# Score units as steps of their own, raw products of the first pair ahead of its maxima, and a new table of numbers behind a planned schedule

## The chip, the cores and the metric

The kernel runs on one core of one Trainium2 chip. The metric is device time in microseconds (us) of one execution; lower is better. A profiled execution also gives a trace of every engine: PE is TensorE (PEld its weight loads), DVE is VectorE, ACT is ScalarE, POOL is GpSimd, SP is the engine from whose queue nearly all DMAs are issued.

## The reference, cut to what matters

Three stages follow each other, all in float32, with B=4, H=8 heads, S=576, D=64, d_model 512, d_ff 1024:

```
scores = q @ k.T / 8, masked by blocks of 64 (block_i >= block_j)
attn   = exp(scores - max) / (sum + 1e-9);   x = attn @ v          # per head
h      = relu(x @ w_in);  conv over time with 3 taps per channel
x      = (h * sigmoid(conv)) @ w_out                               # first feed-forward stage
h      = relu(x @ w_in2); u, v = halves;  v_n = layer norm of v
x      = (u * (w_spatial @ v_n + b_spatial)) @ w_out2              # second feed-forward stage
```

## The kernel before

Heads are worked in 16 pairs, four to a batch. For a pair p these steps run on PE, and each leaves a task for the other engines:

- `max_step` (line 519, four per pair): rounded products of keys and queries in whole-array matmuls, only to find each row's maximum; DVE reduces them from PSUM into `mx` (lines 535 and 542). `max_tr` (line 555) turns `mx` over; the result is copied to `mt` (line 567 on ACT or 569 on DVE) and sent by two small DMAs into row 0 of each half of `mq` (line 574).
- `score` (line 635): the exact products again, with PE divided into two halves of 64 rows, one per head. `unit` (line 600) makes one PSUM tile: for the first six pairs (`PF32`) float32 products of `raw` (line 613), later three products of split values `kp`, `qbd`, `kl` (line 621), and on top a product of `mk` and `mq` (line 625) that subtracts the maxima and masks. ACT takes the exponential into `e` (line 629). Two calls of `score` per pair make two units each.
- `av` (line 647): products with `v` and with ones, in the divided array (line 323). `norm_b` (line 742) spreads the reciprocal of the sums; DVE multiplies (line 753), POOL rounds the result to `x` (line 326) and the rest goes to the second half of `x` (line 329 on DVE, 333 on POOL).
- `in1` and `out1` (lines 769 and 814): the first feed-forward stage, whole-array matmuls of line 315, in tiles of 12 to 24. ACT, DVE and POOL turn each `in1` tile into a gate `g` (lines 788 to 805); `out1` leaves `y`, which goes out to memory and comes back for the second stage.

Every float32 operand of a whole-array matmul is split into a rounded high part and a low part, the low part being a subtraction: `minus` (line 331) makes it on DVE or on POOL. Weights arrive as 64-bit words and are rebuilt first: `words_to_f32` (line 384) takes the sign on DVE (line 392) or on POOL (line 390), then two shifts on DVE (394, 396); `split64` (line 399) loads and splits one weight unit of 128x512.

The order of all of this is planned when the program is built. `Order` (line 88) plays the engines through time with assumed durations (`t_act`, `t_dve`, `t_round`, `t_ptt`) and instructions stand on each engine in the order in which this play starts them. Whenever its PE is free, `pick_at` (line 896) chooses the next step: maxima, `norm_b`, attention steps or the feed-forward stream, by how far the two streams have come (`AHEAD`). PSUM has three double banks `st` and two single banks `mo` in this phase. A table of numbers at lines 30 to 77 sets thresholds, priorities (`P_...`), start times of the weight loads (`PREP_...`) and bit masks; in a mask, bit p or bit c says which engine takes the work of pair p, weight unit c or tile c.

When attention is done its buffers close, the second stage's weights `w2i` load and are split, and the second stage runs (lines 1028 to 1250).

Of the kernel before, what the change touches and what calls it, by code (L numbers as in the profile page):

```python
# [38 lines left out]
X1KEEP = (1, 2)
PONES = 7  # L40
KL_POOL = 0x4018
QL_POOL = 0x8038
SGN_POOL = 0xf500
M_ACT = 0x9000
Q_DVE = 0x1180
PTWO = 16
P_KL = 1
# [10 lines left out]
EARLY_M = 5
TILE_ON = 0.2
JOIN = 0  # L60
S_FIRST = 6
# [209 lines left out]


def t_round(n):
    return 0.11 + n * 0.00092


def t_ptt(n):
    return 0.15 + n * 0.0021


@with_exitstack
def attn_moe_moe2_kernel(
# [98 lines left out]
    qbd = [att.tile([128, NBLK, 128], F32R, name=f"qbd{i}") for i in range(NKP)]  # L381


    def words_to_f32(r, f, prio, pool=False):
        n = f.shape[-1]
        yield ("ACT", t_act(n, False), lambda: nc.scalar.activation(
            f, r[:, :, 1].bitcast(F32), ACTF.Copy, scale=2.0 ** -112), 0, prio)
        if pool:
            s = r[:, :, 1].bitcast(F32)
            yield ("POOL", t_round(n), lambda: nc.gpsimd.tensor_scalar(s, s, 0.0, None, ALU.mult), 0, prio)  # L390
        else:
            yield ("DVE", t_dve(n, True), lambda: nc.vector.tensor_scalar(
                r[:, :, 1], r[:, :, 1], 0x80000000, None, ALU.bitwise_and), 0, prio, True)
# [4 lines left out]

    def split64(src, hi, lo, key, pool=None, prio=None):
        prio = P_W if prio is None else prio  # L400
        unit = {"w1i": 0, "w1o": 8, "w2i": 16, "w2o": 24}[key[0]] + key[-1] + (4 * key[1] if len(key) > 2 else 0)
# [13 lines left out]
        yield from words_to_f32(r, f, prio, (SGN_POOL >> unit) & 1)  # L415
# [219 lines left out]
    def score(p, g):
        def fn():
            ES[p, g] = att.tile([128, 2, ESZ[g]], F32, name=f"e{g}", tag=f"e{g}", bufs=NE[g])
            if g == 0 and p >= PONES:
                od.spawn(add_up(p), "att")
            tasks = [unit(p, g, i) for i in range(2)]  # L640
            if g == 1 and p >= PF32:
# [778 lines left out]
```

## Time and profile before

| | us |
|---|---|
| median of 3 runs (lowest, highest) | 625.69 (624.18, 626.79) |
| the profiled execution, its device time | 625.44 |
| the profiled execution, span from first to last instruction | 623.7 |
| PE busy in the span | 584.6 |
| DVE, ACT, POOL busy | 469.5, 255.4, 149.2 |

The span and the busy times belong to the profiled execution; 1.7 us of its device time lie outside the span. A busy engine is one with an instruction in flight. PE's matmuls overlap, so short gaps between them do not show as idle.

### The profile page before, as it was taken

The numbers are of one execution on the slowest core, as the hardware profiler recorded it, in microseconds if no ns is written. First come the engines' busy times: TensorE is split into PE (matmuls) and PEld (weight loads), VectorE is DVE, ScalarE is ACT, GpSimd is POOL, SyncE is SP. The second block draws the span as 40 slices with busy tenths as digits, with TensorE's granted clock in tenths as the row PEclk, the third lists the DMA queues.
The fourth block names the chain that finished last, engine by engine and source line by source line (L and its number), as shares of the span: only waits on it lengthen the run. The fifth ranks groups of instructions, "written<-read, shape, count | busy, mean of one in ns | idle before, by whom it ended". The sixth has DMA issues, their size and how long they took to land.

```text
span 623.7 us, 12021 instructions
## 1 busy us (share of the span) xinstructions
PE 584.6 (94%) x4638; PEld 524.4 (84%) x4638; DVE 469.5 (75%) x1010; ACT 255.4 (41%) x516; POOL 149.2 (24%) x202
## 2 busy tenths in 40 slices
PE   5888799899999999999999999799999999999997
PEld 4655578798879978979788999798889999998997
DVE  6799979796987967969948498888794577258257
ACT  4556554633524715527336273636333013103101
POOL 6012133430351201306242130222121122012011
PEclk9999999999999999999999999999999999999999
DMA  5656521313121023040010285435700600510012
GB/s 172 196 173 189 175 79 30 127 39 102 41 96 61 2 98 99 2 136 3 23 58 21 75 257 145 134 102 153 228 1 16 215 20 0 173 56 2 1 58 76
DMA packets 41927, 56.65 MB, mean 91 GB/s; under 512 B 9381, under 2 KB 34725, under 8 KB 41870
## 3 DMA queue, kind: packets, MB, share of 16 engines
q1 hardware_dynamic: 41182, 55.69, 28.4%
q8 instruction: 36, 0.59, 0.4%
q0 software_dynamic: 400, 0.16, 0.1%
q14 instruction: 21, 0.17, 0.1%
q10 hardware_dynamic: 288, 0.04, 0.0%
HBM read 41.42 MB, written 14.16 MB: 89 GB/s over the span
## 4 chain that ended last, share of the span: by engine, by line
PE 49%; DVE 28%; DMA 8%; issue 7%; POOL 4%; ACT 3%; SPq 1%; ACTq 0%; POOLq 0%; DVEq 0%
PE mo L315 27%; PE st L315 12%; PE st L323 5%; DVE cc L795 5%; DVE mx L542 4%; DVE cc L800 3%; DVE es L689 2%; DVE kl L329 2%; DVE g L329 2%; DMA w_raw<-in_w2i_dram 2%; PE st L621 2%; PE st L613 2%; DMA w_raw<-in_w1o_dram 2%; DMA w_raw<-in_w1i_dram 2%; POOL g L326 1%
## 5 line engine op out<-in xcount | busy, mean ns | idle before, releaser
L315 PE MATMUL mo<-x,w1i_h 128*128 128x290 f32 x488 | 105.5, 300 | 4.9 <-ACT h L788 4.1
L315 PE MATMUL mo<-g,w1o_h 128*128 128x288 f32 x416 | 89.9, 299 | 2.6 <-DVE y L833 2.6
L315 PEld LDWEIGHTS mo<-x,w1i_h 128*128 128x128 f32 x488 | 80.9, 189 | 7.3 <-ACT h L788 5.1
L326 POOL TENSOR_SCALAR g<-cc 128x288 fp32r<-128x288 f32 x64 | 38.7, 608 | 186.2 <-DVE cc L800 178.5
L795 DVE SCALAR_TENSOR_TENSOR cc<-h,cwt,cc 128x288 f32<-128x288 f32 x128 | 67.2, 539 | 8.6 <-ACT cc L792 8.0
L315 PEld LDWEIGHTS mo<-g,w1o_h 128*128 128x128 f32 x416 | 68.8, 189 | 5.5 <-DVE y L833 3.9
L315 PE MATMUL mo<-x,w1i_l 128*128 128x290 f32 x244 | 72.4, 297 | 0.0
L315 PE MATMUL mo<-g,w1o_l 128*128 128x288 f32 x208 | 61.4, 295 | 0.0
L629 ACT ACTIVATE e<-st 128x640 f32<-128x640 f32 (+1 forms) x64 | 50.8, 833 | 17.6 <-PE st L625 9.9
L323 PE MATMUL st<-e,v 128*64 128x448 f32 (+4 forms) x384 | 48.4, 402 | 7.0 <-DVE mx L542 5.1
L315 PE MATMUL mo<-x,w2i_h 128*128 128x288 f32 x256 | 52.6, 296 | 1.6 <-ACT u L1092 1.5
L323 PEld LDWEIGHTS st<-e,v 128*64 128x64 f32 x384 | 25.5, 139 | 31.7 <-issue 16.6
L326 POOL TENSOR_SCALAR gt<-ga 128x288 fp32r<-128x288 f32 x40 | 21.0, 524 | 116.2 <-DVE ga L1117 74.2
L542 DVE TENSOR_REDUCE mx<-st 128x1 f32<-128x320 f32 (+6 forms) x100 | 44.8, 483 | 3.0 <-PE st L315 2.8
L315 PEld LDWEIGHTS mo<-x,w1i_l 128*128 128x128 f32 x244 | 46.1, 189 | 0.1
L315 PEld LDWEIGHTS mo<-x,w2i_h 128*128 128x128 f32 x256 | 41.4, 188 | 2.7 <-ACT u L1092 2.6
L792 ACT ACTIVATE cc<-h,cwt 128x288 f32<-128x288 f32 x64 | 33.6, 535 | 18.4 <-DVE g L329 14.3
L315 PE MATMUL mo<-ws_h,vnh 128*128 128x288 f32 x135 | 39.6, 297 | 1.4 <-issue 1.1
L797 ACT ACTIVATE cc<-cc 128x288 f32<-128x288 f32 x64 | 27.8, 441 | 31.8 <-DVE cc L795 30.8
L329 DVE TENSOR_TENSOR gt<-ga,gt 128x288 fp32r<-128x288 f32 x56 | 25.0, 468 | 19.8 <-POOL gt L326 19.8
L315 PE MATMUL st<-w2i_h,x 128*128 128x512 f32 x128 | 39.5, 390 | 0.0
L315 PEld LDWEIGHTS mo<-g,w1o_l 128*128 128x128 f32 x208 | 39.1, 188 | 0.1
(168 smaller groups left out, 1460.3 us busy)
## 6 DMA issues: line engine op xcount, KB each, us to landing
x2d<-y SPq DMA_DIRECT2D x32, 288.0 KB
x<-x2d SPq DMA_DIRECT2D x16, 576.0 KB
raw<-in_kq_dram SPq DMA_DIRECT2D x15, 576.0 KB
v<-in_vt_dram SPq DMA_DIRECT2D x16, 320.0 KB
out_dram<-o SPq DMA_DIRECT2D x32, 144.0 KB
w_raw<-in_w1i_dram SPq DMA_DIRECT2D x8, 512.0 KB
w_raw<-in_w1o_dram SPq DMA_DIRECT2D x8, 512.0 KB
w_raw<-in_w2i_dram SPq DMA_DIRECT2D x8, 512.0 KB
```

The lines of the kernel that those rows point to most:

```text
L315: nc.tensor.matmul(o, w, x, start=start, stop=stop)
L323: nc.tensor.matmul(o[row:row + m], w, x, start=start, stop=stop)
L326: nc.gpsimd.tensor_scalar(o, i, 1.0, 0.0, ALU.mult, ALU.add)
L329: nc.vector.tensor_tensor(o, a, b, ALU.subtract)
L542: yield ("DVE", t_dve(n), lambda: nc.vector.tensor_reduce(mx[:, c:c + 1], st[bk][:, o:o + n], AX.X, ALU.max), 0, 0)
L613: nc.tensor.matmul(out, keys(RAW[p][:, 0, :], r), RAW[p][r, 1, q0:q0 + nq], start=True, stop=False)
L621: nc.tensor.matmul(st[:, e, o:o + nq], keys(kx, slice(64 * e, 64 * e + 64)), qx[e], start=j == 0, stop=False)
L629: yield ("ACT", t_act(2 * n), lambda: nc.scalar.activation(ex[:, :, e0:e0 + n], st[:, :, 0:n], ACTF.Exp, scale=0.125), 0, 0)
L792: yield ("ACT", t_act(HT, False, 1), lambda: nc.scalar.activation(cc, h[:, o:o + HT], ACTF.Copy, scale=cwt[:, c, 1:2]), 0, P_G)
L795: yield ("DVE", t_dve(HT, ptr=1), lambda: nc.vector.scalar_tensor_tensor(cc, h[:, o + e:o + e + HT], cwt[:, c, j:j + 1], cc, ALU.mult, ALU ...
L797: yield ("ACT", t_act(HT, False), lambda: nc.scalar.activation(cc, cc, ACTF.Tanh, scale=0.5), 0, P_G)
L800: yield ("DVE", t_dve(HT), lambda: nc.vector.scalar_tensor_tensor(cc, cc, 1.0, h[:, o:o + HT], ALU.add, ALU.mult), 0, P_G, True)
```

## The change

1. `score` makes one unit per step instead of two, so that `pick_at` can put another step between the two units of a call.
2. For pair 0 the first two units are cut in two: their raw products (line 613 before) are a step that needs only the loaded data, the product with the maxima is a second step.
3. `stay`: when PE is in the divided array and an attention step lacks nothing but a PSUM bank or its margin, the planner waits up to `STICK` = 0.1 us for it.
4. The planner's durations of ACT and POOL work are changed.
5. Almost the whole table of numbers is new: which engine takes which work, priorities, when weights load, how the streams are interleaved.

```diff
-AHEAD = (0.58, 0.27, 0.16, 0.37)
-PREP_AT = 18
+AHEAD = (0.47, 0.62, 0.22, 0.75)
+PREP_AT = 8
...
-W_DVE = 0xffffff7
+W_DVE = 0x6fd08
...
 def t_round(n):
-    return 0.11 + n * 0.00092
+    return 0.317 + n * 0.00056
 def t_ptt(n):
-    return 0.15 + n * 0.0021
+    return 0.31 + n * 0.0019
...
-    def unit(p, g, i):
+    HALF = {}
+    def unit(p, g, i, part=None):
         n, parts, et, e0 = SSTEPS[g][i]
         q, ex = mq[p % NQ], ES[p, et]
-        st = two_banks()
+        st = HALF.pop((p, g, i)) if part == 1 else two_banks()
+        if part == 0:
+            HALF[p, g, i] = st
...
-                if p < PF32:
+                if p < PF32 and part != 1:
                     nc.tensor.matmul(out, keys(RAW[p][:, 0, :], r), RAW[p][r, 1, q0:q0 + nq], start=True, stop=False)
...
-            for e in range(2):
+            for e in range(2 if part != 0 else 0):
                 r = slice(64 * e, 64 * e + 64)
                 nc.tensor.matmul(st[:, e, o:o + nq], keys(mk, r), q[r, q0:q0 + nq], start=False, stop=True)
...
-    def score(p, g):
+    def score(p, g, i, part=None):
...
+        if part == 0:
+            return dict(needs=[("raw", 0, 0), ("raw", 0, 1)], rings=[("st", 1)] + ([(f"e{g}", 1)] if i == 0 else []), fn=fn, tile=True)
+        if part == 1:
+            return dict(needs=[("m", p)], rings=[], fn=fn, tile=True)
...
+        if p == 0:
+            sstream.extend(score(p, 0, i, part) for part in range(2) for i in range(2))
+        sstream.extend(score(p, g, i) for g in range(p == 0, 2) for i in range(2))
...
+    def stay():
+        if not od.tile or od.t - od.pe_free >= STICK:
+            return False
+        if ready("v", vstream, 0.0) or ready("s", sstream, 0.0) or not (due("s", sstream) or due("v", vstream)):
+            return False
+        od.push(od.t + 0.05, lambda: None)
+        return True
...
     def pick():
+        if stay():
+            return None
```

Three places show what this does to the order.

The first is PE from the end of pair 0's maxima. `mo` and `st` are PSUM tiles, `qbd_97` and `qbd_98` the queries of pairs 0 and 1, `raw` the loaded data, `ident` marks the turning of the maxima. Before:

```order
L315 MATMUL st<-kp,qbd_97 128x288 x2
L561 MATMUL st<-ident,mx 9x128
L315 MATMUL mo<-kp,qbd_98 128x64
L315 MATMUL mo<-kp,qbd_98 128x128
L315 MATMUL mo<-kp,qbd_98 128x192
L315 MATMUL mo<-kp,qbd_98 128x256
L315 MATMUL st<-kp,qbd_98 128x320
L315 MATMUL st<-kp,qbd_98 128x384
L315 MATMUL st<-kp,qbd_98 128x448
L315 MATMUL st<-kp,qbd_98 128x512
L613 MATMUL st<-raw 128x320 x2
L625 MATMUL st<-mq_94,mk 128x320 x2
```

Now:

```order
L619 MATMUL st<-raw 128x320 x2
L316 MATMUL st<-kp,qbd_97 128x320
L316 MATMUL st<-kp,qbd_97 128x384
L619 MATMUL st<-raw 128x256 x2
L316 MATMUL mo<-kp,qbd_97 128x448
L316 MATMUL mo<-kp,qbd_97 128x512
L316 MATMUL st<-kp,qbd_97 128x288 x2
L562 MATMUL st<-ident,mx 9x128
```

Two pairs of raw products have moved from behind eight products of pair 1 to a place ahead of the turning of pair 0's maxima.

The second is POOL after its first copies. `qbd` are rounded queries, `x` the rounded attention output of a pair, `w_raw` the sign of a weight unit, `w1i_l` and `w1o_l` low parts of weights. Before:

```order
L333 TENSOR_TENSOR w1i_l<-w_f,w1i_h 128x4x128
L326 TENSOR_SCALAR x_538<-xpair 128x576
L326 TENSOR_SCALAR qbd_98<-raw 64x9x64
L326 TENSOR_SCALAR x_700<-xpair 128x576
L390 TENSOR_SCALAR w_raw<-w_raw 128x512
L326 TENSOR_SCALAR qbd_97<-raw 64x9x64
L326 TENSOR_SCALAR x_859<-xpair 128x576
L390 TENSOR_SCALAR w_raw<-w_raw 128x512 x2
L326 TENSOR_SCALAR x_1018<-xpair 128x576
L390 TENSOR_SCALAR w_raw<-w_raw 128x512 x2
```

Now:

```order
L391 TENSOR_SCALAR w_raw<-w_raw 128x512
L334 TENSOR_TENSOR w1i_l<-w_f,w1i_h 128x4x128 x2
L327 TENSOR_SCALAR qbd_98<-raw 64x9x64
L334 TENSOR_TENSOR w1i_l<-w_f,w1i_h 128x4x128 x2
L327 TENSOR_SCALAR qbd_97<-raw 64x9x64
L334 TENSOR_TENSOR w1i_l<-w_f,w1i_h 128x4x128 x2
L327 TENSOR_SCALAR x_557<-xpair 128x576
L327 TENSOR_SCALAR qbd_98<-raw 64x9x64
L334 TENSOR_TENSOR w1i_l<-w_f,w1i_h 128x4x128
L327 TENSOR_SCALAR x_707<-xpair 128x576
L334 TENSOR_TENSOR w1o_l<-w_f,w1o_h 128x512
```

The subtractions of seven `w1i` units and one `w1o` unit stand on POOL where one stood, and the signs have gone back to DVE but for one.

The third is SP's queue behind the first loads. `mq_94` and `mq_95` are the rows of maxima of pairs 0 and 1. Before:

```order
L949 DMA cwr<-in_cw_dram 128x48
L511 DMA v<-in_vt_dram 128x640 x2
L574 DMA mq_94<-mt 1x9x64
L459 DMA raw<-in_kq_dram 128x1152
L411 DMA w_raw<-in_w1i_dram 128x4x256
L574 DMA mq_95<-mt 1x9x64
```

Now:

```order
L982 DMA cwr<-in_cw_dram 128x48
L512 DMA v<-in_vt_dram 128x640
L412 DMA w_raw<-in_w1i_dram 128x4x256
L512 DMA v<-in_vt_dram 128x640
L575 DMA mq_94<-mt 1x9x64
L412 DMA w_raw<-in_w1i_dram 128x4x256 x2
L460 DMA raw<-in_kq_dram 128x1152
L412 DMA w_raw<-in_w1i_dram 128x4x256
L575 DMA mq_95<-mt 1x9x64
```

Four loads of weights are issued ahead of the second pair's row of maxima, where one was.

## Rows read from the trace of the kernel before

**Rows 1.** The page's span, and its first part: busy us, share, instructions.

```profile
span 623.7 us, 12021 instructions
...
PE 584.6 (94%) x4638; PEld 524.4 (84%) x4638; DVE 469.5 (75%) x1010; ACT 255.4 (41%) x516; POOL 149.2 (24%) x202
```

**Rows 2.** Windows: stretch, length, busy us (instructions) per engine, clock, DMA share, GB/s.

```profile
0.00:15.00 15.00, 8.08 (x32) 6.21 (x33) 10.38 (x29) 6.54 (x12) 9.46 (x20) 1.00 0.53 179
15.00:75.00 60.00, 48.77 (x513) 34.48 (x514) 53.06 (x124) 35.72 (x55) 9.58 (x10) 1.00 0.59 177
75.00:120.00 45.00, 42.02 (x428) 33.47 (x424) 36.52 (x76) 25.00 (x48) 13.86 (x12) 0.96 0.31 100
120.00:345.00 225.00, 217.77 (x1828) 193.45 (x1829) 181.45 (x363) 101.09 (x204) 65.31 (x79) 1.00 0.17 54
345.00:480.00 135.00, 128.00 (x868) 121.37 (x867) 104.83 (x225) 62.83 (x141) 28.17 (x40) 1.00 0.42 127
480.00:624.00 144.00, 139.93 (x978) 135.43 (x977) 83.27 (x195) 24.20 (x58) 22.85 (x42) 1.00 0.21 67
```

**Rows 3.** PE's waits from 15 to 75: total us, times, longest.

```profile
PE st L323 <- DVE mx L542: 4.4, 3, 1.6
PE st L315 <- ACT e L629: 3.1, 3, 1.2
PE st L315 <- DVE mt L569: 1.6, 1, 1.6
PE st L323 <- ACT e L629: 1.4, 2, 1.0
```

**Rows 4.** PE's waits from 75 to 345.

```profile
PE mo L315 <- DVE y L833: 2.6, 5, 0.8
PE st L315 <- DVE srow L714: 2.2, 1, 2.2
...
PE st L561 <- DVE mx L542: 0.9, 1, 0.9
```

**Rows 5.** PE's waits from 345 to 480.

```profile
PE mo L315 <- ACT h L788: 3.2, 2, 1.8
...
PE mo L315 <- DVE y L833: 0.8, 1, 0.8
```

**Rows 6.** DVE, timeline at the start: start, us, instruction, idle before it.

```profile
18.14 0.28 DVE L569 CAST mt<-st 9x128 fp32r<-9x128 f32 x1 [1.91 <-PE st L561]
...
23.94 0.44 DVE L392 TENSOR_SCALAR w_raw<-w_raw 128x512 uint32<-128x512 uint32 x1 [1.96 <-ACT w_f L386]
```

**Rows 7.** Groups by form: busy us, mean ns of one, idle before.

```profile
L329 DVE TENSOR_TENSOR g<-cc,g 128x288 fp32r<-128x288 f32 x52 | 29.7, 576 | 6.5 <-POOL g L326 6.4
...
L333 POOL TENSOR_TENSOR g<-cc,g 128x288 fp32r<-128x288 f32 x12 | 11.5, 955 | 0.9
...
L390 POOL TENSOR_SCALAR w_raw<-w_raw 128x512 f32<-128x512 f32 x6 | 10.4, 1740 | 15.6 <-ACT w_f L386 15.6
...
L392 DVE TENSOR_SCALAR w_raw<-w_raw 128x512 uint32<-128x512 uint32 x22 | 10.2, 463 | 7.8 <-ACT w_f L386 7.6
...
L329 DVE TENSOR_TENSOR kl<-raw,kp 128x576 fp32r<-128x576 f32 x9 | 8.7, 965 | 0.1
...
L329 DVE TENSOR_TENSOR w1i_l<-w_f,w1i_h 128x512 fp32r<-128x512 f32 x7 | 4.8, 683 | 0.2 <-ACT w1i_h L420 0.2
...
L333 POOL TENSOR_TENSOR kl<-raw,qbd 64x576 fp32r<-64x576 f32 x2 | 3.4, 1702 | 0.2
```

**Rows 8.** POOL alone, groups by form.

```profile
L333 POOL TENSOR_TENSOR w1i_l<-w_f,w1i_h 128x512 fp32r<-128x512 f32 x1 | 1.3, 1277 | 3.7 <-ACT w1i_h L420 3.7
```

**Rows 9.** The tile `g`: shortest, median and longest ns of DVE's subtraction.

```profile
L329 DVE TENSOR_TENSOR g<-cc,g x52: 432/452/2375, 100.8 to 406.0; 128x288 fp32r<-128x288 f32 x52
```

**Rows 10.** DVE's waits over the span, for the sign of weights on POOL.

```profile
DVE w_raw L394 <- POOL w_raw L390: 7.1, 3, 2.7
```

**Rows 11.** SP's queue at 307 us: the issue of one row of maxima.

```profile
307.11 0.76 SPq L574 DMA_DIRECT2D mq<-mt  x1
```

More of the change, by code (lines that the diff above doesn't have):

```diff
@@ L29 @@
 NEG = -(2.0 ** 30)
-AHEAD = (0.58, 0.27, 0.16, 0.37)
-PREP_AT = 18
+AHEAD = (0.47, 0.62, 0.22, 0.75)
+PREP_AT = 8
 PREP_DT = 2.5
-PREP_DT2 = 5
-PREP_AT2 = 46
+PREP_DT2 = 2.5
+PREP_AT2 = 36
 NKP = 2
@@ L38 @@
 PF32 = 6
-X1KEEP = (1, 2)
+X1KEEP = (0, 1)
 PONES = 7
[L41 to L47, printed above, removed]
+KL_POOL = 0xbe22
+QL_POOL = 0xaa37
+SGN_POOL = 0x1
+M_ACT = 0xd8c6
+Q_DVE = 0x0
+PTWO = 5
+P_KL = 2
 NPR = 0
 SPLIT = 2
-GLO_POOL = (192, 197, 0, 36, 8, 129, 64, 0)
-W_DVE = 0xffffff7
-P_KPQ, P_RAW, P_V, P_G, P_W = 1, 0, 1, 1, 3
-X1_POOL = 0x10a0
-CWP = 0
+GLO_POOL = (225, 117, 200, 165, 56, 76, 104, 144)
+W_DVE = 0x6fd08
+P_KPQ, P_RAW, P_V, P_G, P_W = 0, 0, 1, -1, 2
+X1_POOL = 0x8328
+CWP = 1
 NX1 = 6
@@ L57 @@
 NRAW = 3
[L58 to L61, printed above, removed]
+EARLY_M = 2
+TILE_ON = 0.3
+JOIN = 0.01
+S_FIRST = 2
 HOLD = 1
-STKEEP = 0
+STKEEP = 2
 MARGIN = 0.4
-EARLY = 2
-WPRIO = 3
+STICK = 0.1
+EARLY = 3
+WPRIO = 1
 W2PRIO = 2
-W2DT = 2.0
+W2DT = 0.8
 DMA_LAG = 0.8
-ADD_DVE = 0xbfff
-V_ACT = 0xdcfd
-S_ACT = 0x6214
+ADD_DVE = 0xffca
+V_ACT = 0xa77d
+S_ACT = 0x258a
 P_ADD = 0
-XE = (1.0, 2.25)
+XE = (0.5, 1.75)
 XMO = 7
-XK = 0.4
+XK = 0.25
 WR = 2
@@ L158, in enqueue @@
         eng, dur, fn = it[:3]
-        lat = it[3] if len(it) > 3 else 0.0
+        lat = (it[3] if len(it) > 3 else 0.0) + (0.03 if eng == "ACT" else 0.0)
         prio = it[4] if len(it) > 4 else 1
@@ L381, in attn_moe_moe2_kernel, with words_to_f32 @@
     qbd = [att.tile([128, NBLK, 128], F32R, name=f"qbd{i}") for i in range(NKP)]
-    def words_to_f32(r, f, prio, pool=False):
+    def words_to_f32(r, f, prio, sign="DVE"):
         n = f.shape[-1]
-        yield ("ACT", t_act(n, False), lambda: nc.scalar.activation(
+        yield ("ACT", t_act(n, False) + 0.04, lambda: nc.scalar.activation(
             f, r[:, :, 1].bitcast(F32), ACTF.Copy, scale=2.0 ** -112), 0, prio)
-        if pool:
-            s = r[:, :, 1].bitcast(F32)
-            yield ("POOL", t_round(n), lambda: nc.gpsimd.tensor_scalar(s, s, 0.0, None, ALU.mult), 0, prio)
+        s = r[:, :, 1].bitcast(F32)
+        if sign == "POOL":
+            yield ("POOL", 0.2 + 0.003 * n, lambda: nc.gpsimd.tensor_scalar(s, s, 0.0, None, ALU.mult), 0, prio)
         else:
@@ L414, in split64 @@
         f = pool.tile([128, 512], F32, name="w_f", tag="w_f", bufs=2)
-        yield from words_to_f32(r, f, prio, (SGN_POOL >> unit) & 1)
+        yield from words_to_f32(r, f, prio, "POOL" if (SGN_POOL >> unit) & 1 else "DVE")
         if pool is pa:
@@ L622, in unit @@
                                          start=j == 0, stop=False)
-            for e in range(2):
+            for e in range(2 if part != 0 else 0):
                 r = slice(64 * e, 64 * e + 64)
                 nc.tensor.matmul(st[:, e, o:o + nq], keys(mk, r), q[r, q0:q0 + nq], start=False, stop=True)
-            od.cost += 5 * nq / 2400 + 0.12 if p < PF32 else 4 * max(nq / 2400 + 0.015, 0.105)
+            if part is None:
+                od.cost += 5 * nq / 2400 + 0.12 if p < PF32 else 4 * max(nq / 2400 + 0.015, 0.105)
+            else:
+                od.cost += (4, 1)[part] * nq / 2400 + (0.1, 0.02)[part]
+        if part == 0:
+            return None
         def task():
@@ L633, in unit @@
         return task(), "att"
-    def score(p, g):
+    def score(p, g, i, part=None):
         def fn():
[L637 to L641, printed above, removed]
+            if i == 0 and part != 1:
+                ES[p, g] = att.tile([128, 2, ESZ[g]], F32, name=f"e{g}", tag=f"e{g}", bufs=NE[g])
+                if g == 0 and p >= PONES:
+                    od.spawn(add_up(p), "att")
+            tasks = [unit(p, g, i, part)]
+            if part == 0:
+                return None
+            if (g, i) == (1, 1) and p >= PF32:
                 KPQ.pop(p)
             return tasks
-        return dict(needs=[("m", p)] + ([("kl", p)] if p >= PF32 else []), rings=[("st", 2), (f"e{g}", 1)], fn=fn,
-                    frees=[("mq", 1)] + [("raw", 1)] + ([("kpq", 1)] if p >= PF32 else []) if g == 1 else [], tile=True)
+        if part == 0:
+            return dict(needs=[("raw", 0, 0), ("raw", 0, 1)], rings=[("st", 1)] + ([(f"e{g}", 1)] if i == 0 else []), fn=fn, tile=True)
+        if part == 1:
+            return dict(needs=[("m", p)], rings=[], fn=fn, tile=True)
+        return dict(needs=[("m", p)] + ([("kl", p)] if p >= PF32 else []), rings=[("st", 1)] + ([(f"e{g}", 1)] if i == 0 else []), fn=fn,
+                    frees=[("mq", 1)] + [("raw", 1)] + ([("kpq", 1)] if p >= PF32 else []) if (g, i) == (1, 1) else [], tile=True)
     def av(p):
@@ L849, in attn_moe_moe2_kernel @@
     for p in range(NPAIR):
-        sstream.extend(score(p, g) for g in range(2))
+        if p == 0:
+            sstream.extend(score(p, 0, i, part) for part in range(2) for i in range(2))
+        sstream.extend(score(p, g, i) for g in range(p == 0, 2) for i in range(2))
         vstream.append(av(p))
@@ L884, in next_x @@
     def next_x(margin):
+        if pos["s"] == 0 and pos["x"] > 3:
+            return None
         p, j = divmod(pos["x"], nx)
-        if p >= NPAIR or pos["s"] < 2 * (p - 1) + XK * j - XE[pos["m"] >= EARLY_M]:
+        if p >= NPAIR or (pos["s"] - 2) / 2 < 2 * (p - 1) + XK * j - XE[pos["m"] >= EARLY_M]:
             return None
@@ L1250, in pick2 @@
     def pick2():
+        if stay():
+            return None
         for margin in (MARGIN, 0.0):
```

5 lines of the change are left out of this document (3 added, 2 removed).

## The prediction

> **What bounds the kernel now.** I read the engines' shares first, then the windows, then PE's waits stretch by stretch. PE is busy 584.6 of 623.7 us [rows 1]; the order of both builds has the same 4168 matmuls, so nearly all that can be won lies in 39.1 us of idle time. By stretch [rows 2] it is 6.9 us up to 15, 11.2 from 15 to 75, 3.0 to 120, 7.2 to 345, 7.0 to 480 and 4.1 in the rest. The reader is to see that the shares mislead: DVE is busy 75% over the span, but 53.1 of 60 us between 15 and 75, and 36.5 of 45 behind that. In the early stretch the attention steps of five pairs meet the rebuilding of the weights, and PE waits 10.5 us in four groups: 6.0 us for DVE (4.4 for reduced maxima, 1.6 for the turned ones) and 4.5 us for ACT's exponentials [rows 3]. From 75 to 345 the largest waits are DVE's again, 2.6, 2.2 and 0.9 us [rows 4], yet PE is 97% busy there. From 345 to 480 it is ACT's relu, 3.2 us, then DVE's `y`, 0.8 us [rows 5]. From 480 on PE is full but for the end.
>
> **The change part by part.** The numbers of instructions are counted in the order of both builds, the durations are means [rows 7, 8].
>
> *Work that leaves DVE.* 15 subtractions of `g` at 0.576 us are 8.6 us; 13 of weights (6 `w1i`, 1 `w1o`, 6 `w2i`, one shape) at 0.683 are 8.9; 11 of `kl`, on keys and on queries, at 0.965 are 10.6. Twelve small copies of maxima and reciprocals go to ACT at 0.28 [rows 6]: 3.4 us. Three copies of queries and two subtractions of `x` go to POOL; they have the 576 columns of the `kl` row, so by it 4.8. To DVE come 5 signs at 0.463, 2.3 us, and one set of sums, 2.7 us by its element count from the `kl` row. Net: 36.3 - 5.0 = 31.3 us off DVE.
>
> *What POOL pays.* 15 x 0.955 + 13 x 1.277 + 11 x 1.702 (for both kinds of `kl`) - 5 signs x 1.740 = 14.3 + 16.6 + 18.7 - 8.7 = 40.9 us, on an engine that is busy 149.2 [rows 1]. It stays under a third of the span; what it costs is delay and contention. DVE's subtraction of `g` has a median of 452 ns, a mean of 576 and a longest of 2375 [rows 7, 9]: 52 x 0.124 = 6.4 us were lost beside POOL's present work. If all two-input work suffers by as much again for 27% more POOL time, DVE loses about 2 us; if every added microsecond of POOL blocks DVE, 40.9. I take 4, near the row, and keep 27 us of the 31.3.
>
> The Trainium skill, page "SBUF — State Buffer", section "Who interferes with whom", speaks against the change here: a DVE instruction with two SBUF inputs contends with a GpSimd one that reads SBUF, and whoever comes second is blocked for the whole instruction. The longest `g` agrees with such blocking, the median says that most escape. By the rule at its hardest the 31.3 would turn into a loss of 9.6; that is the second rival below.
>
> *The start.* Raw products for 576 columns go ahead of the turned maxima, into time in which PE waits for DVE's reductions, and pair 0's first two units then need only the product with `mq`. That shortens the way to pair 1's turned maxima by about 1 us, which is part of the 1.91 us for which DVE stood idle [rows 6]. But pair 1's turned maxima are now copied by ACT, behind the last exponential of pair 0, and two weight units stand on DVE ahead of pair 2's reductions. The time of pair 1's row is then the same within a microsecond. I count 0 (-1.0 to +1.0). What does change is that the weights are planned from 8 us instead of 18 and fill DVE's idle 1.91 and 1.96 us.
>
> *15 to 75.* Of the 29.8 us this stretch and the 15 us behind it get: six `w1i` subtractions (4.1), seven small copies (about 2.0), one `x` and one query copy (1.9), less five signs (2.3), so 5.7 us, and 3.9 us of idle DVE are used. DVE also stops waiting 7.1 us for signs on POOL [rows 10], mostly behind 75. PE's waits for DVE here are 6.0 us; those for ACT stay. I take three quarters, -4.5. At best all 11.2 us go; at worst the denser weight work (unit every 2.5 us instead of 5 for `w1o`) puts the shifts in front of reductions and costs 3.
>
> *75 to 345.* PE's DVE waits shown are 5.7 us, all idle 10.2. Some 16 us come off DVE here. PE is already 97% busy and the tight ones are latencies, not throughput, so I take half of the 5.7: -3. Bounds: -10 and +8. The `mo` banks alone now carry the feed-forward stream, so two banks must turn over per 1.6 us tile; no cost by the waits shown, since ACT's relu cost PE little before 345.
>
> *345 to 480.* Six `w2i` subtractions leave DVE (4.1 us), and loads are asked for every 0.8 us instead of 2.0, but PE waits here for ACT. -1, between -4 and +4.
>
> *Rows of maxima.* For the last 11 pairs both rows go through SP, one issue of 0.76 us more [rows 11]. It is hidden by the feed-forward tiles that the order keeps between a turning and its scores from pair 6 on; uncovered it is 11 x 0.76 = 8.4 us. Taken: +0.2.
>
> *Staying in the divided array.* Runs of one array form rise from 75 to 77 in the order, so `stay` saves no switch. From 120 to 345 all of PE's idle is 7.2 us over roughly 50 switches, under 0.15 us each: +0.3 for two.
>
> Sum: 0 - 4.5 - 3 - 1 + 0.2 + 0.3 = -8.0 us. Against the profiled execution, 625.44 us (span 623.7 and 1.74 around it), that is 617.4; the median of the runs shown is 0.25 higher, so I predict 617.7.
>
> **The rivals.**
>
> *DVE's relief goes deeper.* The same terms at two thirds of their best: -7.5, -6.5, -2.5 and nothing against, 609. For it: DVE's 88% from 15 to 75. Against: 4.5 us there are ACT's, and ACT gets more copies.
>
> *The lock eats it.* Every POOL subtraction blocks a DVE one for its whole length. From 15 to 75, seven new ones of 1.277 us cost 8.9 against 5.7 + 3.9 won, and behind that POOL's 32 us outweigh what leaves DVE; only the second stage's 1 us is left: 625. For it: the longest `g`. Against: the median.
>
> *POOL's queue delays the gates: slower.* POOL works in order. For six late pairs a subtraction of `kl` on keys now stands there, for four of them with both halves of the queries, 1.7 x 3 = 5.1 us in front of the rounding and subtraction of a `g` that `out1` needs. Where `out1` is next on PE that is exposed: 4 x 5.1 less one tile of 1.6 us each = 14 us, with the early gain kept 625.4 - 4.5 + 14 = 635; half exposed, 628. It decides as soon as a `g` is less than 5 us ahead of its use. For it: gates now have the highest priority but POOL cannot be interrupted. Against: no wait for `g` is among PE's waits, and the order keeps `in1` tiles between.
>
> *The change does not do what it says*: the switches do not fall, already in the sum.
>
> **How the numbers follow.** The forecast has 0.58, the deeper relief 0.14, the lock 0.14, POOL's queue 0.14. This kernel's measurement cannot tell less than 0.5%, 3.1 us, from no change. Of the forecast's 0.58 (its own range 612 to 623) I give 0.05 to within that bound; with the lock's 0.14 less 0.03 that lands slower, and 0.03 of POOL's queue, same is 0.19, slower 0.14, faster 0.67. The range of 8 in 10 goes from 608 to 630: below it deeper relief in full, above it POOL's queue in full.
>
> **What would show it.** DVE busy near 443 us, POOL near 190; PE's idle between 15 and 75 down from 11 to about 6.5, with reduced maxima nearly gone from its waits and ACT's exponentials left; the median of `g` on DVE still about 0.45 us. The forecast is wrong if PE waits on `g` or on `mq`, if DVE's two-input means rise by a fifth, or if the idle time from 120 to 345 grows.

## The result, and the profile after

The changed kernel takes 608.51 us (median of 4 runs, 608.11 to 608.88) against 625.81 us before: a ratio of 0.9712, 95% interval 0.9671 to 0.9753. That is 17.3 us, where the forecast had 8.0. The direction was right, the size less than half of what came.

The page after, its span and first part, to be read against [rows 1]:

```profile
span 606.3 us, 11995 instructions
PE 583.5 (96%) x4638; PEld 524.0 (86%) x4638; DVE 452.8 (75%) x963; ACT 257.9 (43%) x528; POOL 188.0 (31%) x237
```

The span is 17.4 us shorter, PE's busy time only 1.1. So 16.3 us are idle time that went, and DVE's share is 75% as before: a share that stays says nothing about the engine's part.

The windows after, in the columns of [rows 2]:

```profile
0.00:15.00 15.00, 8.11 (x25) 5.05 (x25) 8.12 (x24) 5.97 (x11) 9.43 (x20) 1.00 0.64 213
15.00:75.00 60.00, 55.42 (x549) 37.92 (x553) 55.67 (x128) 39.97 (x66) 18.78 (x17) 1.00 0.59 187
75.00:120.00 45.00, 42.41 (x435) 36.03 (x428) 40.76 (x83) 25.41 (x53) 15.11 (x18) 1.00 0.24 74
120.00:345.00 225.00, 224.31 (x1904) 202.54 (x1903) 165.33 (x333) 102.56 (x211) 83.28 (x92) 1.00 0.19 60
345.00:480.00 135.00, 130.64 (x891) 124.34 (x889) 108.39 (x226) 61.29 (x136) 40.67 (x52) 1.00 0.46 144
```

The windows are fixed in time, so the later ones hold somewhat different work in each kernel. Length less PE's busy time gives the idle time: 4.6 us from 15 to 75 (11.2 before), 2.6 to 120 (3.0), 0.7 to 345 (7.2), 4.4 to 480 (7.0). The clock of 0.96 between 75 and 120 has become 1.00. From 120 to 345 PE idles 0.7 us in 225. Together with the stretch up to 120, 6.9 of 10.2 idle us went there, inside the forecast's bounds (-10 to +8) but more than twice its -3.

PE's waits after, from 15 to 75, answering [rows 3]:

```profile
PE st L316 <- DVE mt L570: 2.0, 3, 0.8
PE st L316 <- DVE mx L543: 1.3, 1, 1.3
PE st L316 <- ACT e L640: 0.9, 2, 0.5
PE st L619 <- DVE xpair L720: 0.8, 1, 0.8
```

From 75 to 345, answering [rows 4]:

```profile
PE st L316 <- DVE srow L732: 1.3, 1, 1.3
PE st L562 <- DVE mx L550: 0.9, 1, 0.9
PE mo L316 <- ACT h L806: 0.6, 2, 0.4
PE mo L316 <- DVE y L851: 0.3, 1, 0.3
```

The view of before behind [rows 4] has more waits for DVE than were shown there:

```profile
PE st L561 <- DVE mx L549: 0.9, 1, 0.9
PE st L323 <- DVE mx L542: 0.8, 2, 0.4
PE st L315 <- DVE mx L542: 0.6, 1, 0.6
PE st L561 <- DVE mx L535: 0.5, 1, 0.5
PE st L323 <- DVE xpair L753: 0.3, 1, 0.3
```

So from 75 to 345 PE waited 8.8 us for DVE before, not 5.7, and 2.5 after. From 15 to 75 its waits for DVE fell from 6.0 to 4.1 us. But those for ACT's exponentials fell more there, 4.5 to 0.9, and ACT was given more work, not less (busy 40.0 us instead of 35.7). That alone casts doubt on an account by DVE's relief.

What moved, answering [rows 7, 9]; the last row gives shortest, median and longest ns:

```profile
L330 DVE TENSOR_TENSOR g<-cc,g 128x288 fp32r<-128x288 f32 x37 | 19.7, 539 | 2.2 <-POOL g L327 2.2
L334 POOL TENSOR_TENSOR g<-cc,g 128x288 fp32r<-128x288 f32 x27 | 25.7, 953 | 2.1
L813 DVE SCALAR_TENSOR_TENSOR cc<-h,cwt,cc 128x288 f32<-128x288 f32 x128 | 73.2, 585 | 10.2 <-ACT cc L810 9.6
L395 DVE SCALAR_TENSOR_TENSOR w_raw<-w_raw 128x512 uint32<-128x512 uint32 x28 | 22.2, 793 | 0.3
L330 DVE TENSOR_TENSOR g<-cc,g x37: 440/447/1659, 99.9 to 389.9; 128x288 fp32r<-128x288 f32 x37
```

### The profile page after: what moved, and what is told of

Its sections match the earlier page's. It is cut to its first block, busy times and chain, and to the rows that moved or that the text cites. A ratio compares the mean times of both kernels' runs of the same rounds, so it can differ in the third digit from the quotient of the medians.

```text
span 606.3 us, 11995 instructions
## 1 busy us (share of the span) xinstructions
PE 583.5 (96%) x4638; PEld 524.0 (86%) x4638; DVE 452.8 (75%) x963; ACT 257.9 (43%) x528; POOL 188.0 (31%) x237
## 3 DMA queue, kind: packets, MB, share of 16 engines
q1 hardware_dynamic: 41380, 55.72, 28.8%
## 4 chain that ended last, share of the span: by engine, by line
PE 60%; DVE 24%; DMA 6%; ACT 4%; issue 3%; POOL 2%; SPq 1%; DVEq 0%; POOLq 0%; ACTq 0%
PE mo L316 37%; PE st L316 12%; PE st L324 5%; DVE cc L813 4%; PE st L627 4%; DVE w_f L397 2%; DVE mx L543 2%; DVE w_raw L395 2%; DVE cc L818 2%; DMA rc<-srow 2%; DMA w_raw<-in_w2i_dram 1%; PE st L631 1%; DMA w_raw<-in_w1i_dram 1%; DVE g L330 1%; DVE w_raw L393 1%
## 5 line engine op out<-in xcount | busy, mean ns | idle before, releaser
L316 PE MATMUL mo<-g,w1o_h 128*128 128x288 f32 x496 | 105.4, 298 | 1.5 <-DVE y L851 1.4
L316 PEld LDWEIGHTS mo<-g,w1o_h 128*128 128x128 f32 x496 | 81.6, 189 | 3.4 <-DVE y L851 1.9
L813 DVE SCALAR_TENSOR_TENSOR cc<-h,cwt,cc 128x288 f32<-128x288 f32 x128 | 73.2, 585 | 10.2 <-ACT cc L810 9.6
L316 PE MATMUL mo<-g,w1o_l 128*128 128x288 f32 x248 | 73.4, 296 | 0.0
L640 ACT ACTIVATE e<-st 128x640 f32<-128x640 f32 (+1 forms) x64 | 52.1, 834 | 28.5 <-PE st L631 27.9
L543 DVE TENSOR_REDUCE mx<-st 128x1 f32<-128x320 f32 (+7 forms) x98 | 43.7, 479 | 6.8 <-PE st L316 6.7
L316 PEld LDWEIGHTS mo<-g,w1o_l 128*128 128x128 f32 x248 | 46.6, 188 | 0.2
L324 PE MATMUL st<-e,v 128*64 128x448 f32 (+4 forms) x384 | 46.7, 393 | 0.0
L330 DVE TENSOR_TENSOR gt<-ga,gt 128x288 fp32r<-128x288 f32 x56 | 25.5, 475 | 17.4 <-POOL gt L327 17.4
```

Source lines behind the costliest of these rows:

```text
L316: nc.tensor.matmul(o, w, x, start=start, stop=stop)
L324: nc.tensor.matmul(o[row:row + m], w, x, start=start, stop=stop)
L330: nc.vector.tensor_tensor(o, a, b, ALU.subtract)
L543: yield ("DVE", t_dve(n), lambda: nc.vector.tensor_reduce(mx[:, c:c + 1], st[bk][:, o:o + n], AX.X, ALU.max), 0, 0)
L640: yield ("ACT", t_act(2 * n), lambda: nc.scalar.activation(ex[:, :, e0:e0 + n], st[:, :, 0:n], ACTF.Exp, scale=0.125), 0, 0)
L813: yield ("DVE", t_dve(HT, ptr=1), lambda: nc.vector.scalar_tensor_tensor(cc, h[:, o + e:o + e + HT], cwt[:, c, j:j + 1], cc, ALU.mult, ALU ...
```

## The experiments

JOINT is the theory that the planned order is what gains: its numbers are taken to fit each other, so that an engine's load matters little by itself. The first rival (RELIEF): work off DVE gains, on any order, as the forecast priced it. A second rival (FIT): any disturbance of such an order loses. The expectations below, written before each run, call RELIEF "DVE". They also weigh ORDER (in e1 to e4 the new durations and thresholds), STEPS (the finer steps) and THRESHOLDS (the numbers between the streams). JOINT is what ORDER stands for from e5 on; in e1 to e4 DVE, ORDER and STEPS had each missed at least once.

All runs of whole kernels stand in one table. "Idle" is PE's, in the windows worked out as above, and the clock is the mean granted one, both of the profiled execution. Each ratio is against the kernel before as it ran beside that kernel, with medians of 625.1 to 626.8 us.

| kernel | median us | ratio (95%) | idle | 15–75 | 120–345 | clock |
|---|---|---|---|---|---|---|
| before | 625.8 | 1 | 39.1 | 11.2 | 7.2 | 0.997 |
| changed | 608.5 | 0.9712 (0.9671–0.9753) | 22.8 | 4.6 | 0.7 | 0.999 |
| e1_old_steps | 628.0 | 1.0041 (1.0016–1.0067) | 36.7 | 9.5 | 9.3 | 0.994 |
| e2_new_steps | 652.5 | 1.0411 (1.0387–1.0435) | 47.6 | 6.1 | 22.7 | 0.963 |
| e3_masks_only | 644.6 | 1.0276 (1.0237–1.0316) | 45.1 | 8.6 | 17.2 | 0.971 |
| e4_old_masks | 626.5 | 0.9993 (0.9969–1.0017) | 32.1 | 5.6 | 8.3 | 0.986 |
| e5_after_order_old_engines | 611.6 | 0.9780 (0.9761–0.9799) | 23.5 | 6.6 | 1.4 | 0.993 |
| e6_before_order_new_engines | 633.6 | 1.0129 (1.0103–1.0154) | 43.6 | 11.2 | 10.6 | 0.992 |
| e7_raw_behind | 607.7 | 0.9708 (0.9684–0.9732) | 22.6 | 4.6 | 0.7 | 1.000 |
| e8_old_durations | 622.8 | 0.9951 (0.9936–0.9967) | 30.1 | 3.9 | 8.1 | 0.991 |
| e9_old_thresholds | 617.1 | 0.9852 (0.9808–0.9895) | 28.4 | 5.5 | 5.6 | 0.994 |
| e10_old_weight_times | 621.1 | 0.9915 (0.9880–0.9950) | 31.2 | 6.3 | 7.6 | 0.989 |
| e11_after_touched | 609.2 | 0.9720 (0.9674–0.9766) | 22.1 | 3.8 | 0.3 | 0.994 |
| e12_before_touched | 625.0 | 0.9969 (0.9946–0.9991) | 36.1 | 10.5 | 7.3 | 0.995 |
| e13_one_copy_moved | 619.6 | 0.9897 (0.9863–0.9930) | 28.7 | 5.6 | 5.9 | 0.989 |

**Code or numbers.** e1 is the changed kernel with the old `score` (two units per step, none ahead of the maxima, no `stay`) under all new numbers; e2 is the new code under all old numbers. The core of e1's edit:

```diff
-    def score(p, g, i, part=None):
+    def score(p, g):
-            tasks = [unit(p, g, i, part)]
+            tasks = [unit(p, g, i) for i in range(2)]
-        return dict(needs=..., rings=[("st", 1)] + ([(f"e{g}", 1)] if i == 0 else []), ...
+        return dict(needs=..., rings=[("st", 2), (f"e{g}", 1)], ...
```

> All new numbers and planner durations, but score steps of two units, no raw products ahead of the maxima and no staying in the divided array. Before 625.8, changed 608.5. Theory DVE (the gain is the work moved off DVE) and theory ORDER (the gain is the new durations and thresholds): 608 to 612, since both are kept. Theory STEPS (the gain is the finer score steps): 618 or more.

> The finer score steps, raw products ahead and staying in the divided array, with all old numbers and durations. Theories DVE and ORDER: 623 to 628, PE idle near 39 us. Theory STEPS: 610 to 617, PE idle near 25 us.

Neither half gains alone: the numbers without the steps come out 0.4% longer, the steps without the numbers 4.1%. No theory foresaw 652.5 us for e2. The stretch from 15 to 75 sorts by the steps: the five kernels with the old ones (before, e1, e3, e6, e12) idle 8.6 to 11.2 us there, all with the new ones 3.8 to 6.6. A unit now takes one `st` double bank at a time where a step claimed two; that this is the reason is argued. e1 takes `stay` away as well, so the finer steps and `stay` are not told apart.

**The engines' share of the work.** e3 is the kernel before with only the eleven tables that say which engine does what; e4 is the changed kernel with these set back. In both the order is planned anew.

```diff
-KL_POOL = 0x4018
-QL_POOL = 0x8038
-SGN_POOL = 0xf500
-M_ACT = 0x9000
+KL_POOL = 0xbe22
+QL_POOL = 0xaa37
+SGN_POOL = 0x1
+M_ACT = 0xd8c6
...
-W_DVE = 0xffffff7
+W_DVE = 0x6fd08
```

> The kernel before with only the eleven masks of the change (which engine takes which work); steps, durations, priorities and start times as before. Theory DVE: 611 to 616, DVE busy near 450 us, PE's idle time from 15 to 75 us near 5. Theory ORDER: 622 to 628, the idle time barely moves though DVE is relieved.

> The changed kernel with the eleven masks of before; everything else new. Theory DVE: 618 to 626, most of the gain gone. Theory ORDER: 608 to 613, DVE busy near 470 us again without PE's idle time coming back.

e3 takes work off DVE (busy 463.1 us instead of 469.5) and is 2.8% slower. RELIEF as the forecast used it falls here. But ORDER missed both runs too (622 to 628 and 608 to 613 against 644.6 and 626.5).

To part relief from order, e5 keeps the changed kernel's order of PE to the instruction, but each subtraction runs on the engine that had it before (DVE 464.6 us, POOL 140.5). ACT's and SP's orders stay too; the copies, signs and sums stay on their new engines. e6 is the reverse: the order of PE from before, the subtractions on the new engines.

```diff
-            return ("POOL", t_ptt(n), lambda: nc.gpsimd.tensor_tensor(o, a, b, ALU.subtract), 0, prio, True)
-        return ("DVE", t_dve(n), lambda: sub(o, a, b), 0, prio, True)
+        def fn():
+            (nc.gpsimd if runs_on_pool else nc.vector).tensor_tensor(o, a, b, ALU.subtract)
+            return ("POOL", t_ptt(n), fn, 0, prio, True)
+        return ("DVE", t_dve(n), fn, 0, prio, True)
```

> The changed kernel with PE's order kept row for row; only the subtractions that make low parts run on the engines of before (about 35 back from POOL to DVE). Theory DVE (relief is the gain): 616 to 622, PE's idle time back to 31 or more. Theory ORDER (the order that was planned is the gain, whichever engine subtracts): 608 to 612.

> The kernel before with its PE order kept row for row; only the same subtractions run on the engines of the change (about 35 from DVE to POOL). Theory DVE: 612 to 620. Theory ORDER: 623 to 629. If POOL's slower subtractions delay what PE needs: above 629.

e5's window from 120 to 345, and the longest of PE's waits from 75 to 345:

```profile
120.00:345.00 225.00, 223.57 (x1893) 201.19 (x1892) 175.82 (x359) 102.96 (x211) 60.93 (x73) 1.00 0.18 57
...
PE st L569 <- DVE mx L557: 0.9, 1, 0.9
PE mo L321 <- DVE y L858: 0.7, 2, 0.6
PE st L321 <- DVE mt L577: 0.5, 1, 0.5
```

DVE is 10.5 us busier from 120 to 345 than in the changed kernel (175.8 us; 181.5 before), and PE still idles only 1.4 us there. With two smaller ones its waits for DVE are 2.5 us, as in the changed kernel. The new order with the subtractions on their old engines is worth 13.6 us (625.15 to 611.57 in its own comparison), and the new engines on top 3 to 4 (608.5; by the two ratios 4.3). What copies, signs and sums add was not parted from the order; by the forecast's prices they take about 1 us off DVE (3.4 + 2.9 - 5.0).

On the old order the same subtractions moved cost 8.5 us (e6), and there DVE is not relieved at all. A net 41 subtractions leave it, 28.8 us at their means before, and it stays as busy as it was (469.5). The lines of e6, and the last one for comparison from before:

```profile
PE 589.7 (93%) x4638; PEld 527.3 (83%) x4638; DVE 469.9 (74%) x969; ACT 255.5 (40%) x516; POOL 198.0 (31%) x243
L403 DVE SCALAR_TENSOR_TENSOR w_f<-w_f,w_raw 128x512 uint32<-128x512 uint32 x28 | 25.7, 918 | 0.7
...
L396 DVE SCALAR_TENSOR_TENSOR w_f<-w_f,w_raw 128x512 uint32<-128x512 uint32 x28 | 20.1, 719 | 0.2
```

What stays on DVE takes longer beside the busier POOL. From e5 to the changed kernel the same move frees 11.8 us (464.6 to 452.8) of 27.1. So the relief has no price of its own; it depends on the order that it meets.

**Parts of the order.** e7 puts pair 0's raw products back behind its maxima. e8 to e10 set back one group of numbers each and plan anew: the durations of ACT and POOL work; the thresholds between streams; when weights load.

```diff
# e7
-                if p < PF32 and part != 1:
+                if p < PF32 and part != 0:
# e8, of six lines
-    return 0.317 + n * 0.00056
+    return 0.11 + n * 0.00092
# e9, of ten lines
-AHEAD = (0.47, 0.62, 0.22, 0.75)
+AHEAD = (0.58, 0.27, 0.16, 0.37)
# e10, of six lines
-PREP_AT = 8
+PREP_AT = 18
```

> The changed kernel with the first pair's raw products back behind its maxima; the rest of the order is kept. The forecast counted 0 for them (-1.0 to +1.0): 607.5 to 609.5. If they carry a part of the gain: 611 or more.

> The changed kernel planned with the old durations of ACT and POOL work; steps, table and engines are the new ones, so only the order differs. Theory ORDER: 618 to 640, idle time and half-clock stretches back. Theory DVE: 608 to 612, since the relief is the same.

> The changed kernel with the twelve old numbers that interleave the two streams (AHEAD, TILE_ON, JOIN, S_FIRST, HOLD, STKEEP, EARLY_M, EARLY, XE, XMO, XK, X1KEEP); all else new. Theory THRESHOLDS (this group carries what the steps do not): 618 or more, and the idle time comes back between 120 and 345 us, 7 or more of it. If another group carries it: 607 to 612. Theory FIT (one table fits one order, any part put back loses) also says 618 or more, here and in the next run.

> The changed kernel with the eight old numbers that say when weights load and in what priority (PREP_AT, PREP_DT, PREP_DT2, PREP_AT2, WPRIO, W2PRIO, W2DT, CWP); all else new. Theory THRESHOLDS: 607 to 613. Theory FIT: 618 or more. If weights start later, VectorE's idle from 16 to 24 us should be back and the idle of TensorE from 15 to 75 us rise by 1 to 3.

The raw products are worth nothing, as forecast. Each group set back costs 8.6 to 14.3 us, the tables of engines 18.0 (e4) and the steps 19.5 (e1): 73 us of losses for a gain of 17.3. They overlap. The last two are each needed for the whole gain, and no group carries it alone. e10 refutes THRESHOLDS (607 to 613); e9 missed its 618 or more by 0.9 us, and idles 5.6 us from 120 to 345 where 7 or more were expected.

e11 and e12 touch one threshold of the changed kernel and of the kernel before (`AHEAD` 0.62 to 0.60, and 0.27 to 0.29).

> The changed kernel with one number moved a little: AHEAD of the second batch 0.60 for 0.62. It means nothing by itself but changes the order from there on. Theory FIT: 612 to 625. Theories that a group of numbers or a piece of code carries the gain: 607 to 610.

> The kernel before with one number moved a little: AHEAD of the second batch 0.29 for 0.27. Theory FIT: above 629 more likely than not, since before was fitted too; theories that a group carries the gain: 624 to 628.

609.2 and 625.0: neither moves more than 0.4% from its own kernel, though in the built programs 574 and 545 of PE's 4166 matmuls stand in another place. FIT in its strong form falls; an order survives a small touch.

**What makes the other orders dear.** Four of them (e2, e3, e8, e10) show one wait that no good one has: PE waits 4.1 to 5.3 us at a stretch for a `qbd` of POOL. It is a part of the loss only, since e1 (1.3 us) and e4 (none), which lose more than e8 and e10, do without it. e10, PE's timeline at 130 us, then its clock by windows:

```profile
130.47 0.28 PE L631 MATMUL st<-mq,mk 64*128 64x192 f32 x2
135.98 2.61 PE L316 MATMUL st<-kp,qbd 128*128 128x64 f32 x8 [5.22 <-POOL qbd L327]
140.38 0.85 PE L316 MATMUL st<-kp,qbd 128*128 128x288 f32 x2 [1.79 <-DVE mx L543]
141.15 4.70 PE L324 MATMUL st<-e,v 128*64 128x128 f32 x24
...
168.10 2.92 PE L324 MATMUL st<-e,v 128*64 128x128 f32 x24
```

```profile
131.00:136.00 5.00, 0.02 (x1) 0.02 (x1) 4.39 (x7) 2.97 (x5) 4.84 (x2) 0.86 0.31 107
136.00:140.00 4.00, 2.59 (x8) 1.92 (x8) 2.06 (x6) 0.00 (x0) 0.00 (x0) 0.50 0.00 0
140.00:144.00 4.00, 3.62 (x14) 1.82 (x16) 3.88 (x8) 0.00 (x0) 0.00 (x0) 0.50 0.01 4
144.00:149.00 5.00, 4.95 (x60) 3.52 (x56) 3.47 (x4) 2.07 (x4) 4.51 (x3) 0.92 0.24 66
```

PE stands still for 5.2 us, then the granted clock is 0.50, its level of 1.2 GHz, and 24 products take 4.70 us where 24 of the same form take 2.92 at the full clock. Such a wait is paid twice. The table's clock column shows where: e2, with 47.6 us of idle time, has a mean clock of 0.963 and PE busy 603.6 us, 20 more than the changed kernel for as many matmuls.

What POOL and DVE did meanwhile, in the same kernel:

```profile
131.96 3.97 POOL L327 TENSOR_SCALAR qbd<-raw 64x576 fp32r<-64x576 f32 x1
```

```profile
131.84 1.07 DVE L707 TENSOR_TENSOR es<-e,e 128x896 f32<-128x896 f32 x1
132.84 0.74 DVE L330 TENSOR_TENSOR kl<-raw,kp 128x576 fp32r<-128x576 f32 x1
133.51 0.81 DVE L707 TENSOR_TENSOR es<-es,e 128x640 f32<-128x640 f32 x1
134.25 0.67 DVE L330 TENSOR_TENSOR w1o_l<-w_f,w1o_h 128x512 fp32r<-128x512 f32 x1
134.85 0.54 DVE L707 TENSOR_TENSOR es<-es,e 128x384 f32<-128x384 f32 x1
```

A rounding that takes 0.67 us elsewhere lasts 3.97 and ends 0.5 us after DVE's unbroken run of two-input instructions. Theory: POOL gets no turn inside such a run. e13 is e10 with this one rounding on ACT, PE's and DVE's orders the same:

```diff
-                "POOL", t_round(n), lambda: pool_round(dst[1], own[1]), 0, P_KPQ), ...
+                "POOL", t_round(n), lambda: nc.scalar.activation(dst[1], own[1], ACTF.Copy) if p == 9 else pool_round(dst[1], own[1]), 0, P_KPQ), ...
```

> The kernel with the old weight times, order of PE and DVE unchanged, but the rounding of one half of pair 9's queries, which took 3.97 us on POOL and for which PE waited 5.2 us, runs on ACT. Theory (POOL's copy stood still because DVE ran two-input instructions without a break): the copy takes 0.67 us on ACT, behind the two exponentials there, PE starts the pair's products about 1.9 us earlier, its longest wait falls from 5.2 to about 3.3 us, some of the half-clock stretch behind it goes as well; 621.1 becomes 617 to 619.5. Rival (the stall belongs to the plan and not to POOL): another operand of the same products is late next, the wait stays over 4.5 us, 620.5 to 622.

The wait fell to 3.4 us, as the theory had it, now for ACT; the time is 619.6 against 621.1, just outside the 617 to 619.5 expected and, with overlapping intervals, no proof by itself. The half-clock stretch was expected to shrink as well and did not: the clock is 0.50 from 136 to 144 us again, and the 24 products take 5.31 us.

```profile
140.97 5.31 PE L324 MATMUL st<-e,v 128*64 128x128 f32 x24
```

In the profiled executions PE idles 2.5 us less than in e10 (28.7 against 31.2) and is busy 3.0 us longer (590.7 against 587.7). So the standstill was measured alone, in three small kernels that compute nothing of the reference. Each rounds one 64x576 tile on POOL beside n subtractions of 128x576 on DVE:

```diff
# e14 (DVE's order left to the compiler: reductions came between), e15 (order as written: all write one tile)
+            for _ in range(n - 1 if two else 0):
+                nc.vector.tensor_tensor(c, a, b, ALU.subtract)
# e16: a tile of its own for each
+            for j in range(1, n if two else 0):
+                nc.vector.tensor_tensor(c[j], a, b, ALU.subtract)
```

> Nothing of the reference is computed. Only one question: a POOL rounding of 64x576 (0.67 us when undisturbed) starts beside n two-input subtractions of 128x576 on DVE without a break (n = 0, 1, 2, 4, 8; 0.74 us each), or beside 8 one-input reductions. Theory (POOL gets no turn between two-input instructions of DVE): POOL takes 0.67 us at n = 0 and with the reductions, then about 0.67 n + 0.67: 1.4, 2.0, 3.4 and 6.0 us. Rival (POOL is held for one instruction at most): 1.4 us for every n from 1. Second rival (DVE is the one held): POOL stays at 0.67 and the first subtraction behind it takes 1.4.

> The same question, with DVE's instructions kept in the order written, so that its runs have no reduction between them; nothing of the reference is computed. Theory (POOL gets no turn between two-input instructions of DVE): the rounding takes 0.66 us alone and beside 8 reductions, and beside runs of 1, 2, 4 and 8 subtractions about 1.1, 1.8, 3.1 and 5.8 us (0.45 us more than alone beside one, as in the run before, and 0.67 us for each further one). Rival (held for one instruction at most): 1.1 us for each length.

> The run of subtractions again, nothing of the reference computed; the only difference is that each subtraction of a run writes a tile of its own. In the measurement before all wrote one tile, and subtractions then started 0.79 us apart where 0.67 is usual in the kernels, so that a gap lay between them, and POOL took 1.11 us at every length. Theory (POOL gets its turn only in a gap between two-input instructions, and back to back they leave none): beside runs of 1, 2, 4 and 8 it now takes 1.1, 1.8, 3.1 and 5.8 us. Rival (it always gets the next turn): 1.1 us at every length, and the standstills of 4 us in the kernels have another cause, which stays open.

e14 did not ask its question, since no run stayed unbroken: POOL took 0.66 us alone and 1.11 beside a subtraction. In e15, POOL with n = 2, 4 and 8:

```profile
13.90 1.11 POOL L316 TENSOR_SCALAR o<-i 64x576 fp32r<-64x576 f32 x1 [0.57 <-DVE i L313]
16.07 1.11 POOL L316 TENSOR_SCALAR o<-i 64x576 fp32r<-64x576 f32 x1 [1.05 <-DVE i L313]
19.82 1.11 POOL L316 TENSOR_SCALAR o<-i 64x576 fp32r<-64x576 f32 x1 [2.64 <-DVE i L313]
```

And in e16, with n = 0, beside 8 reductions, and with n = 1, 2, 4, 8:

```profile
4.46 0.67 POOL L316 TENSOR_SCALAR o<-i 64x576 fp32r<-64x576 f32 x1 [4.02 <-DVE i L313]
5.69 0.67 POOL L316 TENSOR_SCALAR o<-i 64x576 fp32r<-64x576 f32 x1 [0.57 <-DVE i L313]
12.22 1.12 POOL L316 TENSOR_SCALAR o<-i 64x576 fp32r<-64x576 f32 x1 [5.87 <-DVE i L313]
13.91 1.78 POOL L316 TENSOR_SCALAR o<-i 64x576 fp32r<-64x576 f32 x1 [0.57 <-DVE i L313]
16.26 3.12 POOL L316 TENSOR_SCALAR o<-i 64x576 fp32r<-64x576 f32 x1 [0.57 <-DVE i L313]
19.96 5.80 POOL L316 TENSOR_SCALAR o<-i 64x576 fp32r<-64x576 f32 x1 [0.57 <-DVE i L313]
```

The e15 result went against the theory. There DVE's instructions all wrote one tile, and some 0.04 us lay between them. With a tile each and no gap (e16) POOL is held for the whole run, 0.67 us more for each further instruction; these start 0.67 us apart. That is what was expected (1.1, 1.8, 3.1 and 5.8 us).

## Why the prediction was right or wrong

The forecast's terms came out as 0, -6.6, -6.9 and -2.6 us, with -0.1 in the rest and -1.1 of PE's busy time; that is -17.3 where -8.0 was forecast. The forecast's own range of 612 to 623 missed; its range of 8 in 10, 608 to 630, holds 608.5 at the very edge.

- *Start*, 0 forecast: 6.9 us idle up to 15 before and after. Right; e7 confirms that the raw products bring nothing.
- *15 to 75*, -4.5 forecast: -6.6. The gain came, but not by DVE alone: e1 has the new engines and idles 9.5 us there, e4 the old engines and 5.6. The new code of the steps carries it.
- *75 to 345*, -3 forecast: -6.9 (0.4 up to 120, 6.5 behind). **This is the step that failed**: "PE is already 97% busy and the tight ones are latencies, not throughput, so I take half of the 5.7: -3." The 5.7 added up only the largest waits for DVE; all of them were 8.8, and not half went but all save 2.5. They did not go by relief, by which the forecast priced them, with the order of PE taken as given. The order is what changed: e5 gives DVE its subtractions back, waits for it 2.5 us there all the same and keeps 13.6 of the 17.3 us, while e3 relieves DVE by 6.4 us in another planned order and loses 18.0 (626.63 to 644.62).
- *345 to 480*, -1 forecast: -2.6, with ACT's relu down from 3.2 us to nothing among the largest waits:

```profile
PE mo L316 <- DVE y L851: 1.7, 2, 1.1
PE mo L316 <- ACT u L1125: 1.5, 2, 1.1
PE mo L316 <- issue: 0.9, 1, 0.9
```

- *Clock*, no term: -1.1 of PE's busy time. A window at a clock of 0.57 from 75 to 79 us before has no counterpart.
- *Rows of maxima* and *staying in the divided array*, +0.5 together: no wait for `mq` after, nothing to see of either.
- *The durations behind the sum.* DVE was to be busy 443 us (31.3 off it, less 4 for contention) and is 452.8. `cc` went from 539 to 585 ns (128 x 0.046 = 5.9 us), the last product of the gate from 486 to 524 (2.4), the shift of line 395 from 713 to 793 (2.2). The contention was there, on other instructions than `g`, whose mean fell to 539. `kl` on POOL took 1.42 and 1.45 us instead of 1.70. POOL's 188.0 was forecast as 190. Some figures were misread, with little weight in the sum: six of the eleven `kl` are halves of 64x576, at 802 ns on DVE and not 965; the 29.8 us shared out over the stretches should be the 31.3; and the 4168 matmuls are 4166 in both built programs and 4638 records on both pages.
- *The rivals.* The deeper relief named 609, and its time is the one measured, but by luck: e5 shows another cause. The lock is real: on the old order (e6) it eats DVE's whole relief, as the rival had it, and in the changed kernel 15.3 of 27.1 us. That contention lengthens DVE's instructions is argued there, from e15, where one of them took 1.10 us beside POOL instead of 0.74. What the rival did not have is that POOL stands still as well; the changed kernel has no rounding of `qbd` or `g` over 1.4 us (2.93 before, 4.58 in e8). POOL's queue delaying PE was real in e2, e3, e8 and e10, mostly through `qbd` (through `g` 1.4 us in e3 and 1.3 in e6), and not in the changed kernel.

The Trainium skill, page "SBUF — State Buffer", section "Who interferes with whom", says that whoever issues first holds the shared ports for its instruction and the other waits until that one is finished. The 1.12 us at n = 1 agrees. At n = 8 the measurement goes further: POOL waited for the run and not for one instruction.

What stays open: which feature of the joint order leaves PE 0.7 us of idle time over 225 us. The groups overlap too much to name one, and the priorities were not set back alone. Nor was another table sought for the old steps or the old engines, so that it is not shown that they could not do as well. The planner's new durations of POOL's work are nearer to the trace after: a subtraction of 288 columns is planned as 0.86 us instead of 0.75 (median 0.89), a rounding as 0.48 instead of 0.37 (median 0.60). No kernel here beats the changed one; e7 (607.7) and e11 (609.2) are level with it.

## What to carry to other kernels

Where a schedule is planned from a table, price the order first and the engines' load second: run the new order with the old engines and the old order with the new ones, since here the same move from DVE to POOL was worth 3 to 4 us on one and cost 8.5 on the other. Look whether DVE's busy time falls at all. Do not take a stretch as full because an engine is 97% busy there; ask what each remaining wait is made of, and count it with the slow clock behind it. Keep a POOL instruction that PE needs soon away from an unbroken DVE run of two-input instructions, or break the run (in e14, with a reduction between the subtractions, POOL took 1.11 us).

## What the runs showed of the hardware

- POOL got no turn inside a back-to-back run of two-input DVE instructions: 1.12, 1.78, 3.12 and 5.80 us for a 0.67 us rounding beside runs of 1, 2, 4 and 8 subtractions (e16). Beside 8 reductions from SBUF it took 0.67.
- A gap of some 0.04 us between DVE's instructions (all writing one tile) let POOL in behind the first, 1.11 us at any length; then DVE's next one took 1.10 us instead of 0.74 (e15).
- Moving a net 41 two-input subtractions from DVE to POOL left DVE as busy as before (469.9 us against 469.5, e6) on one order, and freed 11.8 us of 27.1 on another (e5 against the changed kernel).
- After a wait of 5.2 us PE ran at 0.50 of its clock for about 8 us, 1.8 of them another wait, and 24 products took 4.70 us instead of 2.92 (e10). After a wait of 3.4 us they took 5.31 (e13).
